# Output projection and MLP output in four column tiles of 112 instead of two of 224

## The chip, the cores and the metric

The kernel runs on one core of one Trainium2 chip. The metric is the device time of one execution in microseconds (us). A run is one execution; it also leaves a span (first to last instruction) and the mean clock that the throttle granted to the tensor engine. PE is the tensor engine, PEld its weight loads, DVE the vector engine, ACT the scalar engine; SPq and ACTq are the sequencers of Sync and Scalar, which issue the DMAs. A load or store is said to have landed when its semaphore, a counter that other engines wait for, has its sixteenth increment. PSUM is the memory that the matmuls write to.

## The reference, cut to what matters

```python
B, Sq, D = 8, 1, 448;  Hq, Hkv, Sk, Dh = 16, 8, 4096, 256;  F = 1792
# A: decode attention over the last W = 1024 positions of the cache
o = softmax(q @ k^T * Dh**-0.5) @ v           # 8 batches, 16 heads of 256
a = o.reshape(B, Sq, Hq * Dh) @ wo            # wo: 4096 x 448
# B: layernorm, MLP 448 -> 1792 -> 448
b = gelu(layernorm(x) @ w1 + b1) @ w2 + b2
return g * a + (1 - g) * b                    # g: one gate for each batch
```

There are only 8 batches, so a matmul of the output projection has 8 columns of weights (the activations) and streams a 128-row block of `wo` past them.

## The kernel before

Loads go through a ring of nine slots, all issued by Sync: first keys and weights, then keys and values in turn (2 MB each), at the end `wo` in two slots. The last quarter of `wo` comes in three pieces.

```python
OT = 2
DO = D // OT                                            # 224
WO_PARTS = [[(0, NJ8)]] * (NHQ - 1) + [[(0, 4), (4, 6), (6, 8)]]
# ... (cut)
def halves(ps):                                         # L200
    return [(ps[64 * i : 64 * i + NB, :], slice(i * DO, (i + 1) * DO))
            for i in range(OT)]
# ... (cut: attention, MLP hidden layer)
def mlp_out(hs):                                        # at about 32 us
    bb = ps_misc.tile([P, DO], F32, tag="misc", name="bb")
    nc.vector.memset(bb[:], 0.0)
    for c in range(NF):
        w = slot("w2")
        for dst, cols in halves(bb):
            nc.tensor.matmul(dst, lhsT=hs[:, c, :],     # L532
                rhs=w[:, c * D + cols.start : c * D + cols.stop], ...)
    # ... (cut: bias by a matmul of ones)
    nc.vector.tensor_scalar_mul(mixb[:], bb[:], gg_s[:, 1:2])
# ... (cut)
def project(q):
    w = slot("wo", q - q % 2)
    for j in range(NJ8):                                # 8
        o = ((q % 2) * NJ8 + j) * D
        for dst, cols in halves(A_ps):
            nc.tensor.matmul(dst, lhsT=oP[:, j, q, :],  # L594
                rhs=w[:, o + cols.start : o + cols.stop], ...)
# ... (cut)
for q in range(NHQ):                                    # 4 quarters of wo
    project(q)
nc.vector.scalar_tensor_tensor(res[:], in0=A_ps[:], scalar=gg_s[:, 0:1],
    in1=mixb[:], op0=ALU.mult, op1=ALU.add)             # L610
for i, (src, cols) in enumerate(halves(res)):
    eng = nc.sync if i % 2 == 0 else nc.scalar
    eng.dma_start(out_f[:, cols], src)                  # L620
```

The two halves of the output columns lie on partitions 0 to 7 and 64 to 71 of one PSUM tile, so the two matmuls of a pair use different columns of the array.

Of the kernel before, what the change touches and what calls it, by code (L numbers as in the profile page):

```python
# [12 lines left out]
F32 = mybir.dt.float32  # L13
# [4 lines left out]
def kernel(  # L18
# [16 lines left out]
    P = nc.NUM_PARTITIONS  # L35

    NB, Sq, D = A_x.shape
# [14 lines left out]
    FH = F // 2  # L52
    HH = HD // 2
    PAIR = 2
    OT = 2
    DO = D // OT
    QN = 512
    QUAD = 4
# [20 lines left out]
    consts = ctx.enter_context(tc.tile_pool(name="consts", bufs=1))  # L79
# [20 lines left out]
    def done(n=1):  # L100
        consumed[0] += n
        pump()
# [70 lines left out]
    def slot(*key):  # L173
        return slots[index[key]]
# [22 lines left out]

    NX = NR + 2

    def halves(ps):  # L200
        return [
            (ps[64 * i : 64 * i + NB, :], slice(i * DO, (i + 1) * DO))
            for i in range(OT)
        ]

# [9 lines left out]
    qw = consts.tile([P, NJ, NB, Hq // RQ, QUAD, RQ], BF16)  # L215
    oT = consts.tile([P, Hq, NJ, NB], BF16)
    gg = consts.tile([NB, 2], F32)
    spread = consts.tile([NB, OT, 64], F32)
    gg_s = consts.tile([P, 2], F32)
    ones_r = consts.tile([1, NB], BF16)  # L220
    mixb = consts.tile([P, DO], F32)
    res = consts.tile([P, DO], BF16)
# [46 lines left out]
    def norm_and_gate():  # L269
# [18 lines left out]
        for h in range(2):  # L288
# [24 lines left out]
            .rearrange("p (o b) -> p o b", o=1)  # L313
            .to_broadcast([NB, OT, NB]),
        )
# [210 lines left out]
    def mlp_out(hs):  # L526
        bb = ps_misc.tile([P, DO], F32, tag="misc", name="bb")
        nc.vector.memset(bb[:], 0.0)  # L528
        for c in range(NF):
            w = slot("w2")  # L530
            for dst, cols in halves(bb):
                nc.tensor.matmul(  # L532
                    dst,
                    lhsT=hs[:, c, :],
                    rhs=w[:, c * D + cols.start : c * D + cols.stop],
                    start=(c == 0),
                    stop=False,
                )
        for dst, cols in halves(bb):
            nc.tensor.matmul(  # L540
                dst, lhsT=ones_r[:], rhs=b2_r[:, cols], start=False, stop=True
            )
        done()
        nc.vector.tensor_scalar_mul(mixb[:], bb[:], gg_s[:, 1:2])
# [5 lines left out]
    scores(0)  # L550
    top(0)
    mlp_out(hs)
    for u in range(1, NQ):
        transpose_keys(u, steps(u - 1))
# [13 lines left out]
    A_ps = ps_misc.tile([P, DO], F32, tag="misc", name="A_ps")  # L568
# [20 lines left out]
    def project(q):  # L589
        w = slot("wo", q - q % 2)  # L590
        for j in range(NJ8):
            o = ((q % 2) * NJ8 + j) * D
            for dst, cols in halves(A_ps):
                nc.tensor.matmul(  # L594
                    dst,
                    lhsT=oP[:, j, q, :],
                    rhs=w[:, o + cols.start : o + cols.stop],
                    start=(q == 0 and j == 0),
                    stop=(q == NHQ - 1 and j == NJ8 - 1),
                )  # L600
# [6 lines left out]
    for q in range(NHQ):  # L607
        project(q)
# [6 lines left out]
        op0=ALU.mult,  # L615
        op1=ALU.add,
    )
    for i, (src, cols) in enumerate(halves(res)):
        eng = nc.sync if i % 2 == 0 else nc.scalar
        eng.dma_start(out_f[:, cols], src)  # L620

# [29 lines left out]
```

## Time and profile before

| | before |
|---|---|
| time at the start | 194.38 us median of 3 runs (194.11 to 194.55) |
| the profiled execution | 195.04 us, span 193.27 us |
| loaded | 78 MB, mean 403 GB/s |
| matmuls of the projection | 64 of 224 columns |

From the page of before: span, PE's busy time, and of the 40 slices of the span PE's busy tenths, the granted clock in tenths, and the DMA engines' busy tenths.

```profile
span 193.3 us, 4344 instructions
...
PE 151.4 (78%) x1896; PEld 104.9 (54%) x1896; DVE 121.8 (63%) x278; ACT 83.7 (43%) x102; POOL 0.8 (0%) x7
...
PE   1299976898898989889898867887878787937692
...
PEclk9998588899999999999999999999999999975558
DMA  5999999999999999999999999999999999999950
```

The DMA row says that the loads set the pace in nearly the whole span. Only the last slices are free of them. The granted clock is down to 5 tenths in the last but one and back at 8 in the last.

The end of the chain of waits of before (start, length, what was waited for or ran), from 184 us:

```profile
184.52 5.32 PE A_ps L594 x63
189.83 0.03 issue
189.86 0.45 DVE res L610
```

Here the chain is PE's own work, then one vector operation; the stores follow.

The projection (L594) of before in four stretches: PE busy (matmuls), weight loads, granted clock, DMA share, GB/s.

```profile
184.20:187.00 2.80, 2.71 (x30) 2.74 (x32) 0.50 0.59 230
187.00:188.00 1.00, 1.00 (x15) 1.00 (x12) 0.50 0.36 128
188.00:189.00 1.00, 1.00 (x15) 1.00 (x12) 0.51 0.00 0
189.00:190.00 1.00, 0.82 (x16) 0.55 (x12) 1.00 0.00 0
```

PE is never idle in it. But the loads go on until about 188 us, while PE works: the data of the last quarter come late, and PE is slow enough not to notice. And the clock rises at the end: the records put the rise at 188.99 us. Before it a pair of matmuls starts every 187 ns, after it about every 96 ns. At the same clock of 0.50 the query projection (L356) starts a group of four matmuls of 512 columns every 427 ns, which is 0.83 ns a column; 224 columns come to 187 ns, so the two matmuls of a pair do run at the same time.

### The profile page before, as it was taken

How to read it: one execution, taken by the hardware profiler on the slowest of the kernel's cores; microseconds unless marked ns; L12 is line 12 of the kernel's file. 1: busy time of each engine (PE TensorE's matmuls, PEld its weight loads, DVE VectorE, ACT ScalarE, POOL GpSimd, SP SyncE). 2: the span in 40 equal slices, each digit the busy share in tenths (PEclk: the TensorE clock that was granted, in tenths of full speed). 3: DMA queues.
4: the chain of work that ended last, by engine and by line, in shares of the span. 5: the costliest groups of instructions: out<-in, count | busy, mean ns of one | idle time of the engine just before them, and what ended most of it. 6: DMA issues, size and time to landing. Idle time of an engine off the chain costs nothing.

```text
span 193.3 us, 4344 instructions
## 1 busy us (share of the span) xinstructions
PE 151.4 (78%) x1896; PEld 104.9 (54%) x1896; DVE 121.8 (63%) x278; ACT 83.7 (43%) x102; POOL 0.8 (0%) x7
## 2 busy tenths in 40 slices
PE   1299976898898989889898867887878787937692
PEld 0199633666657566564756452737373646413492
DVE  7632313579778787877878685676767676754310
ACT  2343020658638384654828280827272727320000
POOL 1000000000000000000000000000000000000000
PEclk9998588899999999999999999999999999975558
DMA  5999999999999999999999999999999999999950
GB/s 198 414 430 412 452 432 407 429 414 427 431 431 427 434 424 427 420 427 415 434 420 427 422 431 427 424 431 427 420 431 424 427 427 427 424 424 412 415 207 3
DMA packets 6709, 77.97 MB, mean 403 GB/s; under 512 B 913, under 2 KB 1314, under 8 KB 1954
## 3 DMA queue, kind: packets, MB, share of 16 engines
q1 hardware_dynamic: 6496, 77.67, 95.3%
q8 instruction: 15, 0.25, 0.5%
q10 hardware_dynamic: 194, 0.02, 0.1%
q14 instruction: 4, 0.03, 0.0%
HBM read 77.68 MB, written 0.01 MB: 402 GB/s over the span
## 4 chain that ended last, share of the span: by engine, by line
DMA 41%; PE 35%; ACT 12%; DVE 8%; issue 2%; ACTq 0%; DVEq 0%; SPq 0%
DMA slot<-in_A_k_cache_dram 41%; PE ktp L339 10%; PE S_ps L385 7%; ACT kt L342 7%; ACT E L405 5%; PE PO L446 4%; PE A_ps L594 3%; PE sm L471 2%; PE S_ps L356 2%; PE hT L494 2%; PE bb L532 1%; DVE nmx L397 1%; PE hT L484 1%; PE sm L424 1%; DVE EB L413 1%
## 5 line engine op out<-in xcount | busy, mean ns | idle before, releaser
L342 ACT COPY kt<-ktp 128x1024 bf16<-128x1024 bf16 x64 | 63.2, 1017 | 70.7 <-PE ktp L339 70.7
L339 PE MATMUL ktp<-ident,slot 128*128 128x128 bf16 x1024 | 70.3, 224 | 18.9 <-ACT kt L342 11.6
L339 PEld LDWEIGHTS <-slot 128*128 128x128 bf16 x1024 | 64.4, 102 | 26.0 <-issue 17.1
L344 DVE COPY kt<-ktp 128x1024 bf16<-128x1024 bf16 x64 | 41.2, 684 | 11.6 <-PE ktp L339 11.6
L385 PE MATMUL S_ps<-kt,qw 128*8 128x512 bf16 x256 | 32.2, 626 | 0.3 <-DVE qw L375 0.3
L397 DVE TENSOR_REDUCE nmx<-S_ps 128x1 f32<-128x1024 f32 x16 | 19.6, 1224 | 14.8 <-PE S_ps L385 14.8
L413 DVE STREAM_TRANSPOSE EB<-E 128x1024 bf16<-128x1024 bf16 x16 | 19.9, 1246 | 7.8 <-ACT E L405 7.6
L446 PE MATMUL PO<-slot,ET 128*16 128x512 bf16 x256 | 18.4, 410 | 2.3 <-DMA slot<-in_A_v_cache_dram 2.3
L405 ACT ACTIVATE E<-S_ps,nmx 128x1024 bf16<-128x1024 f32 x16 | 17.9, 1119 | 3.3 <-DVE nmx L398 3.3
L385 PEld LDWEIGHTS <-qw 128*8 128x8 bf16 x256 | 7.3, 94 | 14.8 <-issue 10.4
L446 PEld LDWEIGHTS <-ET 128*16 128x16 bf16 x256 | 5.5, 91 | 7.9 <-issue 3.3
L426 DVE CAST ET<-sm 128x256 bf16<-128x256 f32 x16 | 6.6, 414 | 0.7 <-PE sm L424 0.7
L594 PE MATMUL A_ps<-slot,oP 128*8 128x224 bf16 x64 | 5.5, 362 | 0.0
L474 DVE CAST oT<-sm 128x16 bf16<-128x16 f32 x16 | 3.5, 220 | 3.2 <-PE sm L471 3.2
L424 PE MATMUL sm<-selr,ones_f 128*128 128x8 f32 x32 | 5.4, 241 | 0.0
L594 PEld LDWEIGHTS <-oP 128*8 128x8 bf16 x64 | 5.3, 120 | 0.0
L424 PEld LDWEIGHTS sm<-selr,ones_f 128*128 128x128 f32 x32 | 5.0, 195 | 0.5 <-issue 0.4
L421 PE MATMUL sm<-EB,perm 128*128 128x256 bf16 x16 | 4.5, 278 | 0.3 <-DVE oT L474 0.3
L532 PE MATMUL bb<-slot,hs 128*8 128x224 bf16 x28 | 2.6, 368 | 1.9 <-DVE bb L528 1.9
L504 DVE TENSOR_TENSOR z<-hT,b_sb 128x112 f32<-128x112 f32 x1 | 0.3, 274 | 5.5 <-PE hT L494 5.5
L610 DVE SCALAR_TENSOR_TENSOR res<-A_ps,gg_s,mixb 128x224 bf16<-128x224 f32 x1 | 0.5, 451 | 5.0 <-PE A_ps L594 5.0
L356 PE MATMUL S_ps<-slot,xT 128*8 128x512 bf16 x32 | 3.6, 626 | 0.0
(143 smaller groups left out, 89.3 us busy)
## 6 DMA issues: line engine op xcount, KB each, us to landing
slot<-in_A_v_cache_dram SPq DMA_DIRECT2D x16, 2048.0 KB, 36.1
slot<-in_A_k_cache_dram SPq DMA_DIRECT2D x15, 2048.0 KB, 36.1
slot<-in_A_wo_dram SPq DMA_DIRECT2D x3, 896.0 KB, 32.4
slot<-in_A_k_cache_dram SPq DMA_DIRECT2D x2, 1024.0 KB, 6.9
slot<-in_A_wq_dram SPq DMA_DIRECT2D x1, 2048.0 KB
slot<-in_B_w_dram SPq DMA_DIRECT2D x1, 1568.0 KB
slot<-in_B_w_dram SPq DMA_DIRECT2D x1, 1344.0 KB, 9.7
slot<-in_A_wq_dram SPq DMA_DIRECT2D x1, 1024.0 KB
```

What stands on the lines that cost most here:

```text
L339: nc.tensor.transpose(ktp[:, c, :], kn[:, o : o + P], ident[:])
L342: nc.scalar.copy(dst, ktp[:])
L344: nc.vector.tensor_copy(dst, ktp[:])
L356: nc.tensor.matmul(S_ps[32 * t : 32 * t + NB, n * QN : (n + 1) * QN], lhsT=xT[:, r + half, :], rhs=w[:, o + c : o + c + QN], start=(r == 0 ...
L385: nc.tensor.matmul(S_ps[32 * a : 32 * a + RQ, hf * CH * SK : (hf + 1) * CH * SK], lhsT=qw[:, j, b, half, a, :], rhs=KT[hf][:, j, :, a::QUA ...
L397: nc.vector.reduce_max(nmx[:], S_ps[:], axis=AXIS.X, negate=True)
L405: nc.scalar.activation(E[:], S_ps[:], ACT.Exp, bias=nmx[:], scale=1.0, accum_out=rowsum[:])
L413: nc.vector.transpose(EB[:].rearrange("p c r -> p (c r)"), E[:])
L424: nc.tensor.matmul(sm[:, NCK, :], lhsT=ones_f[:], rhs=selr[:], start=True, stop=True)
L426: nc.vector.tensor_copy(ET[:], sm[:, 0:NCK, :])
L446: nc.tensor.matmul(PO[32 * t : 32 * t + PAIR * RQ], lhsT=ET[:, PAIR * c : PAIR * (c + 1), :], rhs=vn[:, PAIR * c * Dh : PAIR * (c + 1) * D ...
L594: nc.tensor.matmul(dst, lhsT=oP[:, j, q, :], rhs=w[:, o + cols.start : o + cols.stop], start=(q == 0 and j == 0), stop=(q == NHQ - 1 and j ...
```

## The change

Its intent: the array can hold four column tiles of 32, and only two are used. With four tiles of 112 columns the projection and the MLP output should stream in half the time; the final vector operation halves its columns. The price is twice the matmul instructions in these two places and four stores instead of two.

```diff
-    OT = 2
+    OT = 4
-    def halves(ps):
+    def tiles(ps):
         return [
-            (ps[64 * i : 64 * i + NB, :], slice(i * DO, (i + 1) * DO))
+            (ps[32 * i : 32 * i + NB, :], slice(i * DO, (i + 1) * DO))
             for i in range(OT)
         ]
-    spread = consts.tile([NB, OT, 64], F32)
+    spread = consts.tile([NB, OT, P // OT], F32)
# ... (cut: the callers of halves, in the MLP output, the projection and
#      the stores, call tiles instead)
```

More of the change, by code (lines that the diff above doesn't have):

```diff
@@ L530, in mlp_out @@
             w = slot("w2")
-            for dst, cols in halves(bb):
+            for dst, cols in tiles(bb):
                 nc.tensor.matmul(
@@ L538, in mlp_out @@
                 )
-        for dst, cols in halves(bb):
+        for dst, cols in tiles(bb):
             nc.tensor.matmul(
@@ L592, in project @@
             o = ((q % 2) * NJ8 + j) * D
-            for dst, cols in halves(A_ps):
+            for dst, cols in tiles(A_ps):
                 nc.tensor.matmul(
@@ L617 @@
     )
-    for i, (src, cols) in enumerate(halves(res)):
+    for i, (src, cols) in enumerate(tiles(res)):
         eng = nc.sync if i % 2 == 0 else nc.scalar
```

## The prediction

> What bounds the kernel now. The page shows the DMA engines at 9 tenths in every slice from the second to the 38th (mean 403 GB/s) while PE is busy 78%. So until about 184 us the loads set the pace. At the end the chain of waits differs: from 184.5 us it is PE alone, 63 matmuls of the output projection (5.32 us), then the final vector operation (0.45 us), two stores issued at 190.33 us (0.37 us to issue on Sync, 0.30 on Scalar), landed by 191.75 us, then a fixed ending to 193.3 us.
>
> What the change does.
> (a) Projection: 64 matmuls of 224 columns in two column tiles become 128 of 112 in four. In the trace of before the granted clock there is 0.50 until 188.99 us, and one pair of tiles starts every 187 ns, which is 224 columns at half of 2.4 GHz: the two tiles do run at the same time. The query projection (line 356) shows four tiles at the same time at clock 0.5: 512 columns, 32 matmuls in 3.6 us, about 107 ns each. The Trainium skill, "TensorE: Matmul & The Clock Gate", Part 3, says small-M matmuls in distinct column groups run concurrently; the trace agrees. The same page puts a floor of about 25 ns between matmul starts; but the 16 matmuls of line 578 start within 0.16 us, 10 to 13 ns apart, so issue should not bind. Estimate: 93 ns for a group of four, 32 groups, 3.0 us instead of 5.3, all on the critical path.
> (b) But the data of wo come late. The landings of its last four transfers in the trace: third quarter 186.22 us, first half of the last quarter 187.36, next piece 187.93, last piece 188.49. In before nothing waits for them: PE reaches the last quarter at about 189.0. At the new speed PE reaches them at about 186.0, 187.0, 187.75 and 188.15, so it will wait at each. After 188.49 remain two groups (0.19 us) and the last matmul's latency (0.25 us): PE ends at about 188.9 instead of 189.82. Real gain 0.9 us, not 2.3.
> (c) Final vector operation on 112 columns instead of 224: 16 columns took 0.226 us and 224 took 0.451, so about 0.33: gain 0.12 us.
> (d) Four stores, two per queue. The second on each queue is issued 0.34 to 0.42 us after the first (spacing on the queues in before); the last landing comes that much later: loss 0.4 us.
> (e) MLP output: 28 matmuls (2.6 us at 31.7 to 34.3 us) take about half, but the DMA engines are full there and set the pace: no gain.
> (f) 188 more PE instructions on 3,800: at most one more 16 KB packet.
>
> Sum: -0.9 - 0.1 + 0.4 = -0.6 us: 193.8 us, range 193.1 to 194.4. Faster by over 2%: 1%; within 2%: 98%; slower: 1%.
>
> What would show it. Projection groups about 93 ns apart at clock 0.5; new PE waits on the transfers of wo in the list of waits; end of projection at 188.9, with DMA traffic ending near 188.0 as before; the final vector operation at 0.33 us; last store landing about 1.8 us after that operation ends (1.45 before).
>
> What would make it wrong. If four tiles do not overlap at 112 columns, PE stays at 5.3 us and the change loses 0.3 us. If the loads end at another time, (b) moves too. If second stores hide behind the first's landing, the gain is 1 us.

## More of the kernel before

The profiled execution took longer than any of the three timed ones.

## The result, and the profile after

| | before | after |
|---|---|---|
| median us | 194.25 (194.11 to 194.55, 4 runs) | 194.22 (194.12 to 194.32, 4 runs) |
| ratio, 95% interval | 1 | 0.9996 (0.9979 to 1.0014) |
| profiled execution, time / span | 195.04 / 193.27 us | 194.13 / 192.26 us |

A ratio here is the mean time of one kernel's fast runs over that of the other's of the same rounds, so not quite the ratio of the medians quoted. The runs of different sessions were on different chips, and before's median moved from 194.25 to 195.08 us between them; only kernels of one session are compared by time.

The forecast time, 193.8 us, was 0.4 below the median measured, inside the range. But two facts do not fit together: the two profiles differ by 1.0 us, the times by nothing that can be told from noise.

The page of after, the lines that answer to those of before:

```profile
span 192.3 us, 4534 instructions
...
PE 150.7 (78%) x1990; PEld 104.7 (54%) x1990; DVE 121.5 (63%) x278; ACT 83.9 (44%) x102; POOL 0.9 (0%) x7
...
PE   1199976999898988979888589896969697837672
...
PEclk9998597899999999999999958999999999985558
DMA  5999999999999999999999999999999999999970
```

The end of the chain of waits of after, from 184 us:

```profile
170.07 18.62 DMA slot<-in_A_wo_dram
188.70 0.04 issue
188.74 0.30 PE A_ps L594 x8
189.04 0.02 issue
189.06 0.33 DVE res L610
```

The 5.32 us of PE work have gone from the chain. In their place stands a transfer of `wo` that was issued at 170.07 us and landed at 188.70. The projection has turned from work into a wait.

The projection of after on the timeline of PE (start, us, then what; in brackets the idle time just before and its releaser):

```profile
184.47 1.69 PE L594 MATMUL A_ps<-slot,oP 128*8 128x112 bf16 x63
186.44 0.92 PE L594 MATMUL A_ps<-slot,oP 128*8 128x112 bf16 x32 [0.29 <-DMA slot<-in_A_wo_dram]
187.61 0.91 PE L594 MATMUL A_ps<-slot,oP 128*8 128x112 bf16 x24 [0.26 <-DMA slot<-in_A_wo_dram]
188.74 0.27 PE L594 MATMUL A_ps<-slot,oP 128*8 128x112 bf16 x8 [0.21 <-DMA slot<-in_A_wo_dram]
```

Half of the projection (64 matmuls) takes 1.7 us: the four tiles do overlap. Then PE stops for each of the last transfers. The third line hides a fourth stop at 188.17 us, which is filled by the modelled ends of matmuls.

The same stretches as shown of before (PE busy, weight loads, clock, DMA share, GB/s):

```profile
184.20:187.00 2.80, 2.29 (x92) 2.08 (x96) 0.50 0.69 266
187.00:188.00 1.00, 0.74 (x32) 0.54 (x22) 0.50 0.40 147
188.00:189.00 1.00, 0.77 (x24) 0.28 (x15) 0.79 0.04 13
189.00:190.00 1.00, 0.01 (x3) 0.00 (x0) 1.00 0.00 0
```

PE idles now in stretches in which it was wholly busy before. The loads end at about the same time (last landing 188.70 us, 188.49 before).

The tail can be cut into five pieces that add up to the span. They are worked out from the records of landings and instructions in each trace (us; "last landing" is the semaphore's sixteenth increment for the last piece of `wo`):

| trace | clock rises | last landing | to PE's end | to the end of the vector op | to the last store's landing | to the end of the span | span |
|---|---|---|---|---|---|---|---|
| before | 188.99 | 188.49 | 1.33 | 0.49 | 1.45 | 1.51 | 193.27 |
| after | 188.41 | 188.70 | 0.31 | 0.38 | 1.83 | 1.04 | 192.26 |

The span is 1.01 us shorter: 1.02 from PE's end, 0.11 from the vector operation and 0.47 from the very last piece, less 0.38 from the later stores and 0.21 from a later landing. The gain in the last piece had not been foreseen at all.

### The profile page after: what moved, and what is told of

It reads as the page before. It is cut to its first block, busy times and chain, and to the rows that moved or that the text cites. A ratio compares the mean times of both kernels' runs of the same rounds, so it can differ in the third digit from the quotient of the medians.

```text
span 192.3 us, 4534 instructions
## 1 busy us (share of the span) xinstructions
PE 150.7 (78%) x1990; PEld 104.7 (54%) x1990; DVE 121.5 (63%) x278; ACT 83.9 (44%) x102; POOL 0.9 (0%) x7
## 4 chain that ended last, share of the span: by engine, by line
DMA 51%; PE 29%; ACT 12%; DVE 5%; issue 1%; ACTq 0%; DVEq 0%; SPq 0%
DMA slot<-in_A_k_cache_dram 21%; DMA slot<-in_A_v_cache_dram 20%; DMA slot<-in_A_wo_dram 10%; PE ktp L339 9%; PE S_ps L385 8%; ACT kt L342 7%; ACT E L405 4%; PE PO L446 3%; PE S_ps L356 2%; PE hT L494 2%; PE hT L484 1%; PE sm L471 1%; PE bb L532 1%; DVE nmx L397 1%; PE sm L424 1%
## 5 line engine op out<-in xcount | busy, mean ns | idle before, releaser
L339 PE MATMUL ktp<-ident,slot 128*128 128x128 bf16 x1024 | 72.8, 229 | 19.3 <-ACT kt L342 10.4
L339 PEld LDWEIGHTS <-slot 128*128 128x128 bf16 x1024 | 67.1, 105 | 25.9 <-issue 15.5
L594 PE MATMUL A_ps<-slot,oP 128*8 128x112 bf16 x128 | 3.8, 287 | 0.8 <-DMA slot<-in_A_wo_dram 0.8
L594 PEld LDWEIGHTS <-oP 128*8 128x8 bf16 x128 | 2.9, 116 | 1.6 <-issue 1.6
L405 ACT ACTIVATION_READ_ACCUMULATOR E<-S_ps,nmx 128x1 f32 x16 | 3.2, 202 | 0.0
```

Source lines behind the costliest of these rows:

```text
L339: nc.tensor.transpose(ktp[:, c, :], kn[:, o : o + P], ident[:])
L405: nc.scalar.activation(E[:], S_ps[:], ACT.Exp, bias=nmx[:], scale=1.0, accum_out=rowsum[:])
L594: nc.tensor.matmul(dst, lhsT=oP[:, j, q, :], rhs=w[:, o + cols.start : o + cols.stop], start=(q == 0 and j == 0), stop=(q == NHQ - 1 and j ...
```

## The experiments

Four theories are named in the expectations. **A**: the profile of before is typical, so the change gains about 0.5 us. **B**: it fell on a slow execution; how long before's projection takes depends on when the granted clock rises, and in most executions it ends nearer to the last landing. Two more came up when the first four runs had shown the last piece of the table: **C**: the end comes 0.45 us later where the store that lands last holds the semaphore that stands second in a closing wait of Sync. **D**: that is a matter of having two stores.

### How far does before scatter?

`before_again` is before unchanged, `after_again` is after unchanged.

> The kernel before, unchanged: how far do its executions scatter, and was the profiled one typical? It took 195.04 us, while its timed runs took 194.11 to 194.55. Theory A (the profile of before is typical): the span is again about 193.3 us and the projection ends about 1.3 us after the last landing of wo. Theory B (it fell on an execution about 0.8 us slower than most): the span is near 192.5 us, and the projection ends nearer to the last landing, for instance because the clock rises from 0.5 earlier in the projection.

> The kernel after, unchanged. Theory A: about 0.5 us faster than before in the same rounds (0.997). Theory B: within 0.2 us (0.999 to 1.001). Both: span near 192.3 us, projection ending about 0.3 us after the last landing of wo.

Measured, in the same rounds: before_again 194.36 us median, 193.92 to 195.61; its comparison runs of before 193.87 to 195.45 (11 runs); after_again 194.12, 194.01 to 194.58, ratio 0.998 (0.9954 to 1.0006). The span of before_again's trace is 192.53 us, as theory B had it. Its projection in two of the stretches shown of before:

```profile
187.00:188.00 1.00, 1.00 (x20) 0.98 (x18) 0.77 0.38 135
188.00:189.00 1.00, 1.00 (x24) 0.82 (x18) 1.00 0.01 4
```

The clock is 0.77 and 1.00 here, where it was 0.50 and 0.51 in the first profile: it rose at 187.46 us instead of 188.99. The projection ended 0.50 us after the last landing instead of 1.33. The Trainium skill, "TensorE: Matmul & The Clock Gate", Part 1, says that the clock is granted from an activity window of 3413 ns that runs free of the kernel. The trace agrees: the clock of before fell at 171.92 us and rose at 188.99, and 17.07 us are five such windows. In three other traces of the two-tile projection (before_again, before_four_stores, before_sems_turned) the slow stretch is 13.65 us, four windows, and the clock rises at 187.46, 187.01 and 187.72 us. So where the rise falls in the projection differs from execution to execution of what is nearly the same program. An estimate from the trace: had the clock not risen at all, the last pair of before would have started at about 190.0 us (30 steps of 187 ns after 184.43), and the span would have been about 193.9; had it risen early, PE would wait for data and end 0.4 us after the last landing, and the span would have been about 192.3. The spans of all 33 comparison runs of before, three sessions together, lie between 192.0 and 194.1. Their mean clocks point the same way: of the 13 runs with a span of 193.2 us or more, 11 have a mean clock of 0.926 or less, of the 12 with 192.7 us or less none. When the clock rose in each of them was not traced; the theory is tested below.

### Two stores or four

```diff
 # before_four_stores: before, each half of the output in two stores of 112
+    for p in range(2):                # (cut: indents, and the choice of the queue)
         for i, (src, cols) in enumerate(halves(res)):
-            eng.dma_start(out_f[:, cols], src)
+            n = DO // 2
+            o = cols.start + p * n
+            eng.dma_start(out_f[:, o : o + n], src[:, p * n : (p + 1) * n])
 # after_two_stores: after, two stores left out (result wrong on purpose)
-    for i, (src, cols) in enumerate(tiles(res)):
+    for i, (src, cols) in enumerate(tiles(res)[:2]):
```

> The kernel before with each of its two stores cut into two of 112 columns, two on each queue; nothing else changed. Both theories: the last landing comes 0.35 to 0.4 us later, so the time rises by 0.3 to 0.4 us (1.002). A rival, that second stores hide behind the first: no change.

> The kernel after with only the first two of its four stores; half of the output stays unwritten, so the result is wrong on purpose. Both theories: 0.35 to 0.4 us faster than after. Set against before it shows what the projection alone gains: theory A about 0.9 us (0.995), theory B 0.4 us or less.

Measured: before_four_stores 194.23 us (ratio to before 0.9993, 0.9961 to 1.0026), after_two_stores 194.36 (0.999, 0.9965 to 1.0016). Neither expectation of the time came true. For two fewer stores that is clear of noise: the means of the same rounds are 194.18 us for after with four stores and 194.39 with two, where 0.35 to 0.4 less was expected. For two more stores the interval still holds the expected 1.002, so there the trace has to decide.

| trace | clock rises | last landing | to PE's end | to the end of the vector op | to the last store's landing | to the end of the span | span |
|---|---|---|---|---|---|---|---|
| before_again | 187.46 | 188.58 | 0.50 | 0.49 | 1.45 | 1.51 | 192.53 |
| before_four_stores | 187.01 | 188.43 | 0.40 | 0.49 | 1.83 | 1.04 | 192.19 |
| after_again | not before the end | 188.69 | 0.40 | 0.39 | 1.83 | 1.03 | 192.34 |
| after_two_stores | not before the end | 188.76 | 0.40 | 0.39 | 1.41 | 1.51 | 192.46 |

The landing moves by 0.38 to 0.42 us, just as expected. But the last piece moves the other way by 0.47 us. In these traces the later landing of the stores is real and is given back, whichever the projection. The records of Sync's last instructions show how (start us, duration ns, semaphores waited for; an ordinary listing of the trace's records):

```
before_again (stores on 103, 102)         after_again (stores on 103, 102, 104, 105)
190.011 1034  waits 104, 103              191.11    28  waits 104, 103
191.490   28  waits 105, 102              191.32    28  waits 105, 102
191.569   28  waits 106, 100              191.39    28  waits 106, 100
```

On the left Sync sits out the landing on 103 (191.02 us) within one instruction of 1034 ns, and then 0.445 us pass before the next one starts, though it has nothing to wait for: 105 had landed long ago and 102 at 190.83. On the right 0.18 us pass there.

### Is it the semaphore's place?

```diff
 # before_sems_turned: before, two middle loads of values in two pieces each,
 # so that the stores get the next semaphores of the ring of eight
-            add_kv("v", A_v_cache, u - LAG)
+            add_kv("v", A_v_cache, u - LAG, parts=2 if u - LAG in (2, 3) else 1)
 # after_sems_turned_back: the same in after, with six loads (2 to 7)
```

> The kernel before with two of its middle loads of values cut in two, so that the two stores get the next two semaphores of the ring of eight. In the four-store runs the program ended 1.04 us after the last landing, in the two-store runs 1.51 us. Theory C (the place of the last store's semaphore in the closing waits of Sync: second semaphore of a wait that has to be sat out costs 0.45 us more): here the late semaphores stand first in their waits, the long wait of 1.0 us goes, and the end comes 1.0 to 1.1 us after the last landing; time 0.4 to 0.45 us below before (0.998). Theory D (two stores leave a wait that is itself long, over about 0.9 us, wherever it stands): the end stays 1.5 us after the last landing, time as before.

> The kernel after with six middle loads of values cut in two, so that the store that lands last holds the semaphore that stands second in its closing wait. Theory C (the place counts): the wait of about 1 us shows as a long instruction on Sync and the program ends 1.5 us after the last landing instead of 1.04: 0.4 to 0.5 us slower than after. Theory D (four stores never pay it): as after, within 0.15 us.

Measured: before_sems_turned ends 1.03 us after its last landing, with two stores, and the long instruction is gone, as theory C had it: theory D falls. Its time is 194.42 us, ratio 0.9978 (0.9951 to 1.0004): what it should have gained, but not clear of noise. In after_sems_turned_back the long instruction did come (1034 ns, waiting for 104 and 103), yet the next one starts 42 ns after it, and the end comes 1.08 us after the last landing: theory C falls too. The kernel is slower than its neighbours (195.02 us), but its trace puts that elsewhere: its last landing of `wo` comes at 189.59 us.

So neither the number of stores nor the place of the semaphore alone makes the gap. A gap of the same size, 0.39 to 0.46 us, stands in the trace of before in front of Sync's records 31, 35, 39, 43, 61, 65, 69 and 79 (counted from 0), mostly four records apart; the one at the end is 79. That looks like a cost tied to the position in Sync's instruction stream, but the traces speak against it for the other seven, which stand before loads that also wait for a semaphore of PE: in before_again such gaps stand in front of records 49, 53, 61, 65 and 69, and in before_sems_turned, which has two records more ahead of them, in front of 51, 55, 63, 67 and 71. They go with the loads and not with the position, and may have another cause than the closing one. A rival for the closing gap that no run here separates is the fetching of instructions: the last packet of 8,192 bytes on the instruction queue q14 starts at 192.84 us in before, after the gap, but at 191.48 in after, 183.64 in before_sems_turned and 160.51 in after_sems_turned_back. The cause stays open. What is shown: the gap of 0.44 us is there in the four traces with two stores on the untouched semaphores and in none of the other ten.

### Is the slow clock what four tiles make up for?

```diff
 # before_kept_warm: before, idle matmuls into a free PSUM tile where PE waits
+    def warm(n):
+        d = ps_kt.tile([P, QN], F32, tag="ktp", name="warm")
+        qf = qw[:].rearrange("p j b g a r -> p (j b g a r)")
+        for _ in range(n):
+            nc.tensor.matmul(d[:], lhsT=ident[:], rhs=qf[:, 0:QN], start=True, stop=True)
+    warm(5)
     values(u - 2)
+    warm(10)
     finish(u - 2)
 # ... (cut: warm(2), warm(5) at four later places)
 # after_kept_warm: the same in after
```

> The kernel before with idle matmuls (128x512, into a free PSUM tile) in PE's gaps from about 168 us on, so that the granted clock should not fall to 0.5 before the projection. Theory B (what the projection of before loses depends on when the clock rises): at clock 1.0 one pair of tiles takes 94 ns, the projection needs 3.0 us, waits for the same landings of wo as after does, and ends at 188.8 to 189.0 us in every run: the scatter of before (193.9 to 195.5) shrinks to that of after (0.6 us), median about that of after or up to 0.3 us below. Theory A (the clock has nothing to do with it): projection 4.5 us or more, time as before. If the clock stays at 0.5 all the same, the run says nothing.

> The kernel after with the same idle matmuls. If the landings of wo set the end of the projection, four tiles at clock 1.0 gain only the last groups: PE ends 0.05 to 0.1 us earlier after the last landing than in after; time within 0.15 us of after, and within 0.2 us of before_kept_warm. If four tiles were worth anything beyond standing in for the clock, this would be clearly below before_kept_warm (193.8 us or less).

Measured: before_kept_warm 194.32 us, 193.97 to 194.46, ratio 0.9964 (0.994 to 0.9988). Its comparison runs of before scatter from 193.83 to 195.64. So the scatter falls from 1.8 us (11 runs) to 0.5 (6 runs), as theory B had it. The idle matmuls did not hold the clock up throughout: in this trace it still fell for one window and rose at 184.26 us, just before the projection. The projection (L605 in this kernel) on its timeline, still with two tiles of 224, and its stretches:

```profile
184.79 2.54 PE L605 MATMUL A_ps<-slot,oP 128*8 128x224 bf16 x44
187.54 0.91 PE L605 MATMUL A_ps<-slot,oP 128*8 128x224 bf16 x12 [0.21 <-DMA slot<-in_A_wo_dram]
188.66 0.36 PE L605 MATMUL A_ps<-slot,oP 128*8 128x224 bf16 x4 [0.21 <-DMA slot<-in_A_wo_dram]
```

```profile
184.20:187.00 2.80, 2.32 (x46) 2.14 (x48) 0.99 0.63 244
187.00:188.00 1.00, 0.79 (x16) 0.51 (x11) 1.00 0.34 127
188.00:189.00 1.00, 0.79 (x10) 0.26 (x7) 1.00 0.01 4
```

At clock 1.00 two tiles run into the same waits for `wo` that four tiles run into at 0.50, and PE ends 0.40 us after the last landing. after_kept_warm measured 194.35 us (194.22 to 194.56), ratio 0.9965 (0.9935 to 0.9994), in another session. Its projection on the timeline:

```profile
185.14 0.97 PE L605 MATMUL A_ps<-slot,oP 128*8 128x112 bf16 x63
186.93 0.57 PE L605 MATMUL A_ps<-slot,oP 128*8 128x112 bf16 x32 [0.81 <-DMA slot<-in_A_wo_dram]
188.10 0.37 PE L605 MATMUL A_ps<-slot,oP 128*8 128x112 bf16 x16 [0.60 <-DMA slot<-in_A_wo_dram]
188.67 0.27 PE L605 MATMUL A_ps<-slot,oP 128*8 128x112 bf16 x8 [0.20 <-DMA slot<-in_A_wo_dram]
189.25 0.27 PE L605 MATMUL A_ps<-slot,oP 128*8 128x112 bf16 x8 [0.30 <-DMA slot<-in_A_wo_dram]
```

Four tiles at the full clock end 0.31 us after the last landing (189.21), two tiles 0.40. That 0.1 us is all that four tiles add on PE once the clock is up; each of the two is one trace.

### Is it the landing of wo that holds after back?

```diff
 # after_first_wo_only: after, all quarters read the first slot of wo
 # (wrong on purpose; everything is loaded as before)
-        w = slot("wo", q - q % 2)
+        w = slot("wo", 0)
```

> The kernel after with every quarter of the projection reading the first wo slot, whose data land by 184.2 us; all of wo is loaded as before. Wrong on purpose. If the landings of wo are what holds after back: no gaps in the projection, 32 groups of 93 ns, PE ends at about 187.6 instead of 189.05 us, time 1.4 to 1.5 us below after. If something else does, the time stays within 0.2 us of after.

Measured: 192.79 us (192.62 to 192.99), ratio to before 0.9888 (0.9862 to 0.9913), and 1.5 us below before_kept_warm of the same rounds; after itself was not in them. Its trace: no stops in the projection, which starts at 184.75 and ends at 187.97 us, 3.2 us at clock 0.50. The last lines of its timeline:

```profile
186.71 1.26 PE L594 MATMUL A_ps<-slot,oP 128*8 128x112 bf16 x43
...
188.01 0.33 DVE L610 SCALAR_TENSOR_TENSOR res<-A_ps,gg_s,mixb 128x112 bf16<-128x112 f32 x1 [2.66 <-PE A_ps L594]
```

PE ends 1.08 us before the last landing of `wo` (189.05) instead of 0.3 to 0.4 us after it. So about 1.4 us of what four tiles gain on PE is lost to the landings, and the faster PE did not bring them forward: the last one came at 188.49 us in before, 188.70 in after and 189.05 here. The check of the output passed this run, although two of its four quarters are multiplied with the wrong half of `wo`; an estimate from the scales of the reference's inputs puts the attention's share of the output at about 0.2%. So a passed check says little about the projection in any kernel here.

### Does the MLP part do anything?

```diff
 # after_mlp_two_tiles: after, the MLP output in two tiles of 224 as in before;
 # the mix takes 112 of its columns (wrong on purpose)
-        bb = ps_misc.tile([P, DO], F32, tag="misc", name="bb")
+        bb = ps_misc.tile([P, 2 * DO], F32, tag="misc", name="bb")
 # ... (cut: tiles of 64 partitions and 2 * DO columns)
-        nc.vector.tensor_scalar_mul(mixb[:], bb[:], gg_s[:, 1:2])
+        nc.vector.tensor_scalar_mul(mixb[:], bb[:, 0:DO], gg_s[:, 1:2])
```

> The kernel after with the MLP output in two tiles of 224 as in before; half of its result is dropped, so the output is wrong on purpose. All theories: the loads set the pace at 30 us, so the last landing of wo and the end do not move; time within 0.15 us of after. If the MLP part of the change bought anything it would be up to 1.3 us slower.

Measured: 194.31 us (194.09 to 195.09), ratio to before 0.9966 (0.9935 to 0.9998); after_kept_warm of the same rounds has 0.9965. After itself was not in these rounds. No loss of 1.3 us shows in the median, so the MLP part bought nothing that can be seen. The profiled execution was the slowest of its six (195.09 us), with the last landing at 189.66.

### Two attempts at a better version

`after_wide_stores`: two tiles of after are made to lie on 16 adjacent partitions (24 to 39 and 88 to 103), so that one store takes both.

```diff
-            (ps[32 * i : 32 * i + NB, :], slice(i * DO, (i + 1) * DO))
+            (ps[32 * i : 32 * i + (32 if i % 2 == 0 else NB), :],
+             (0 if i % 2 == 0 else PADB), slice(i * DO, (i + 1) * DO))   # PADB = 24
-                    lhsT=oP[:, j, q, :],
+                    lhsT=oP[:, j, q, lo:32],        # oP, hs, ones_r: zeros in 0:24
+        p0 = 64 * h + PADB
+        eng.dma_start(
+            out_f[:, h * 2 * DO : (h + 1) * 2 * DO].rearrange("b (i n) -> i b n", i=2),
+            res[p0 : p0 + 2 * NB, :])
 # ... (cut: the gates' spread; two loads of values in two pieces as above)
```

> The kernel after with the column tiles placed so that two tiles fill 16 adjacent partitions (the first of each pair by weights padded with 24 zero columns), so that two stores of 16 rows do the work of four; and the semaphores turned as in before_sems_turned. The projection as in after (ends about 0.3 us after the last landing), the last store lands 1.40 to 1.45 us after the final vector operation instead of 1.83, and under theory C the program ends 1.04 us after that: 0.35 to 0.4 us faster than after. Under theory D 1.5 us after that: time as after.

Measured: 194.84 us, ratio to before 0.9995 (0.9971 to 1.0018): no gain. The outputs are right. The projection ends 0.42 us after the last landing, but the stores land 2.17 us after the vector operation instead of 1.41 to 1.47. The issue of the stores on the timeline, first in this kernel (L630 is the store), then in after (two stores on each queue):

```profile
189.98 0.78 SPq L630 DMA_DIRECT2D out_dram<-res  x1
189.98 0.75 ACTq L630 DMA_DIRECT2D out_dram<-res  x1
```

```profile
189.42 0.72 SPq L620 DMA_DIRECT2D out_dram<-res  x2
189.43 0.65 ACTq L620 DMA_DIRECT2D out_dram<-res  x2
```

One wide store takes as long to issue as two narrow ones. And only two late increments reach its semaphore, where the narrow stores have eight: its 16 rows are written by two DMA engines. The Trainium skill, "DMA: Bandwidth & Descriptors", "Why a DMA increments its semaphore by 16 and not by 1", says that the number of engines is the largest one up to 16 that divides the slowest dimension of both access patterns; with 2 blocks on the side of the output and 16 partitions on the other that is 2, so the trace agrees, and the plan had overlooked it. Whether this or the number of rows makes the issue longer was not tested.

`warm_and_turned`: before with the idle matmuls of before_kept_warm and the semaphores of before_sems_turned.

> The kernel before with both: PE kept warm by idle matmuls as in before_kept_warm, and the semaphores of the stores turned as in before_sems_turned. If the two effects are what was found, they add: projection ends about 0.4 us after the last landing of wo at clock 1.0, and the program ends 1.04 us after the last store lands; span about 192.0 us, time 193.8 to 194.0 us with a scatter of about 0.5 us, so 0.2 to 0.3 us below after and 0.6 to 0.9 us below before (0.995 to 0.997).

Measured: 194.09 us (193.60 to 194.33), correct, ratio to before 0.9947 (0.9916 to 0.9978). It is 0.5% faster, the interval clear of 1. In its trace PE ends 0.40 us after the last landing and the program 1.03 us after the last store's: there the two effects add as expected. The median lies 0.1 us above the forecast of 193.8 to 194.0; the last landing in the trace was late (189.05 us), which may be why. In the same rounds after_kept_warm, four tiles with the same idle matmuls, took 194.35 us. This kernel was not run in the same rounds as after, whose ratio was 0.998 (0.9954 to 1.0006); the intervals overlap, so that it beats after is likely but not shown.

## Why the prediction was right or wrong

- **The time, 193.8 us (193.1 to 194.4), 98% for within 2%: right, in part by luck.** Measured 194.22 us, ratio 0.9996 in the first comparison, 0.998 in the second. The forecast difference of -0.6 us was too large; -0.1 and -0.4 us were measured, neither clear of zero. Two terms were wrong in opposite directions: the gain on PE was put 0.8 us too high for a usual execution (b) and the stores 0.5 us too dear (d), and the sum of them was taken off the timed median of 194.38, while the terms were read from an execution of 195.04.
- **(a) Four tiles overlap, 93 ns for a group of four at clock 0.5: right.** Groups of after start 93 ns apart, and the undisturbed projection of after_first_wo_only takes 3.2 us.
- **(b) PE will wait for `wo` and end at about 188.9 us: right for after** (189.01, with stops until 186.44, 187.61, 188.17 and 188.74). **Wrong is the other end of the difference**, "PE ends at about 188.9 instead of 189.82 ... Real gain 0.9 us". 189.82 us was one execution in which the clock rose late. The five other traces of the two-tile projection (three with the slow clock at its start, two kept warm) show 0.40 to 0.50 us from the last landing to PE's end instead of 1.33; after has 0.31 to 0.40. In those the term is worth 0.1 us, in an execution where the clock never rises, by the estimate above, about 1.6. The sign of this was on the table: the profiled execution took 195.04 us, beyond all timed ones, and the clock's rise at 188.99 was read as a property of the kernel.
- **(c) The vector operation at 0.33 us: right** (0.333).
- **(d) "Four stores ... loss 0.4 us": the landing right, the loss wrong.** The last landing comes 1.83 us after the vector operation instead of 1.45, as said. But the term stopped at the landing. From there to the end of the program it took 1.51 us before and 1.04 after, so the term measures -0.1 us, not +0.4. The words "then a fixed ending" held the assumption that failed. Why the gap in Sync is there stays open.
- **(e) MLP output no gain: right, as far as it could be seen.** **(f) At most one more instruction packet: right**: 15 packets on PE's instruction queue before and after.

Where the gain went, then. Four tiles halve the projection on PE. About 1.4 us of that are lost to the landings of `wo`. What remains depends on when the clock rises: by the estimate and the idle matmuls above it is large only in executions in which it rises late, so the change mostly cuts the slow executions off. Of the second session's runs, after's six are all below 194.6 us, while five of before's eleven lie above 194.7.

## What to carry to other kernels

Before a tail is costed from one profile, compare the profiled execution's time with the timed ones, and look where the granted clock rises in it: work that runs at half the clock in one execution may run at full clock in the next. When work that overlaps late transfers is sped up, list their landings first; the gain ends at the last of them, and keeping the engine's clock up with idle matmuls gave as much here without touching the work. A cost that is read off at a landing must be followed to the end of the program: here 0.4 us were given back there.

## What the Trainium skill lacked or had wrong

- "TensorE: Matmul & The Clock Gate", Part 1: it says that starts of matmuls are never less than about 25 ns apart. In the trace of before the last 16 matmuls of L578 (32 columns each, in four column tiles, clock 0.50) start within 0.16 us, 2 to 15 ns from one to the next and 11 on average (the prediction's 10 to 13 was rough). Part 3 of the page has about 4 ns for each tile that runs at the same time as others, so the floor of Part 1 should be said to hold for one tile.
- The same page, Part 1, puts the penalty of the clock's first ramp under 1% of a typical kernel and advises against fitting it. Here a late ramp at the end cost before about 0.9 us of 193 (1.33 us from the last landing to PE's end instead of 0.40), which is also under 1%, but more than the effect of the whole change, and with idle matmuls the scatter of before fell from 1.8 to 0.5 us.
- "DMA: Bandwidth & Descriptors": it tells how the engines of a DMA are chosen, but not how the time to issue one depends on its shape. A store of 16 rows in two blocks took 0.78 us to issue on Sync, one of 8 rows 0.37 us.
- "Runtime: NRT & Kernel Launch", "Instruction fetch mechanics", has refills of each engine's instructions in blocks of 16 KB. The queue q8 agrees (15 packets of 16,384 bytes, enough for PE's instructions), but the four packets during the span on the other instruction queue, q14, are of 8,192 bytes.
- No page has the gap of 0.44 us between two closing instructions of Sync whose semaphores have all landed. It decides here whether the program ends 1.04 or 1.51 us after the last store's landing; its cause was not found.
